# Where a weight starts in a partition: w_gate's even chunks at six new offsets past a multiple of 128 bytes

## The chip, the cores and the metric

The kernel runs on one core of one Trainium2 chip. The metric is the device time of one execution, in microseconds. A profile of one execution records the span from its first to its last instruction, each instruction's start and duration, and what released it.

## The reference

Block-causal attention over q, k and v of shape (8, 8, 576, 64) in float32, followed by a SwiGLU feed-forward layer on the 4608 tokens of 512 features that it gives:

```
scores = q @ k.T / 8, hidden where block(i) < block(j), blocks of 64
attn   = softmax(scores) @ v
x      = attn as (4608, 512)
out    = (silu(x @ w_gate) * (x @ w_val)) @ w_out
```

w_gate and w_val are (512, 1536), w_out is (1536, 512), all in 8-byte floats. The kernel keeps nearly the precision of float32 with a cheaper product type (F32R): each operand is split in a high part and a low part, and a product is the sum of three, high by high, high by low and low by high.

## The kernel before

**Tiles and loops.** The feed-forward layer works on 18 tiles of 256 tokens. The 1536 columns of w_gate and w_val are cut in 12 chunks of 128 columns, and the 512 features in 4 pieces `d` of 128. For each tile, `feed_forward` goes over the chunks in pairs (i, i+1) with i even. `up(i, 0, ...)` makes the gate products of chunk i (12 matmuls: 4 pieces by 3 products, lines 1105, 1106 and 1107) and then of chunk i+1 (12 more); `up(i, 1, ...)` does the same with w_val (24 matmuls). Each of these matmuls loads 128 by 128 weights into the array (the stationary operand, 512 bytes in each partition) and streams 256 columns of x against them (the moving operand, 1024 bytes in each partition, from `xhl`). The down product with w_out (lines 1197 to 1199) has the activations `hhl` as the stationary operand and streams 512 columns of w_out. From the fifth tile on, the 48 up matmuls of a pair stand behind each other on TensorE: 12 with an even gate chunk, 12 with an odd one, 24 with w_val. In the first four tiles the up products are cut in pieces of 3 matmuls, and attention work may stand between the pieces. Attention (lines 416 to 900) fills the time between the pairs.

**Order.** The program's order is not written out: every step is a task with a cost, a rank and buffers, and a planner (`in_order`) places the tasks on the engines before the program is built. The planner knows nothing of addresses within a partition.

**The weights.** All high and low parts of w_gate and w_val lie in SBUF for the whole run, in tiles of a pool with one buffer. `w_at(which, x, i)` gives the part x (0 high, 1 low) of chunk i. The odd chunks of w_gate are in two tiles `g_odd0` and `g_odd1` (high and low), those of w_val in `v_all0` and `v_all1`, and the even chunks of w_gate in `g_even0` and `g_even1`, with 64 bytes of an unused tile named `gap` ahead of them:

```
    half_w, whole_w = [P, NDC, DFF // 2], [P, NDC, DFF]
    g_odd = [const.tile(half_w, F32R, name=f"g_odd{x}") for x in range(2)]
    v_all = [const.tile(whole_w, F32R, name=f"v_all{x}") for x in range(2)]
    const.tile([P, 16], F32, name="gap")
    g_even = [const.tile(half_w, F32R, name=f"g_even{x}") for x in range(2)]
```

In the built program the tiles begin at these bytes of a partition: g_odd 1984 and 14272, v_all 26560 and 51136, all of them 64 past a multiple of 128; g_even 75776 and 88064, both a multiple of 128. All of `xhl`, `hhl` and the five `wo` buffers (w_out, streamed from DRAM) begin at multiples of 128. Within a tile a chunk is four runs of 512 bytes, 3072 bytes apart (6144 in v_all), so each chunk and each piece d keeps its tile's offset past a multiple of 128.

**Who writes and reads the even chunks.** `weight(i, 0)` fills a chunk once: a ScalarE cast of 128x512 writes the high part (line 983), a VectorE subtraction the low part (line 986). Before that, chunks 8 and 10 hold two pieces of w_out for a while (`AWAY`): written by the same two lines, stored to DRAM (line 1005), and streamed by a few down matmuls of the first two tiles. From then on TensorE alone reads them, in all 18 tiles.

Of the kernel before, what the change touches and what calls it, by code (L numbers as in the profile page):

```python
# [7 lines left out]
F32 = mybir.dt.float32  # L8
F32R = mybir.dt.float32r
# [9 lines left out]
def kernel(  # L19
# [21 lines left out]
    P = 128  # L41
# [5 lines left out]
    NDC = DM // P  # L47
    NFC = DFF // P
# [46 lines left out]
    const = ctx.enter_context(tc.tile_pool(name="const", bufs=1))  # L95
# [106 lines left out]
    half_w, whole_w = [P, NDC, DFF // 2], [P, NDC, DFF]  # L202
    g_odd = [const.tile(half_w, F32R, name=f"g_odd{x}") for x in range(2)]
    v_all = [const.tile(whole_w, F32R, name=f"v_all{x}") for x in range(2)]
    const.tile([P, 16], F32, name="gap")
    g_even = [const.tile(half_w, F32R, name=f"g_even{x}") for x in range(2)]

    def w_at(which, x, i):

        if which:  # L210
            return v_all[x][:, :, i * P : (i + 1) * P]
        return (g_odd if i % 2 else g_even)[x][:, :, i // 2 * P : (i // 2 + 1) * P]

# [703 lines left out]
    def weight(i, kind):  # L919
# [16 lines left out]
        def part(j):  # L936
            if wo:
                return wo[0][:, j : j + 1]
            which, c = away or (kind, i)
            return w_at(which, j, c)  # L940
# [130 lines left out]
    def feed_forward(j, t0, w, xs):  # L1071
# [19 lines left out]
        def up(i, which, prev):  # L1091
# [3 lines left out]
            for y in range(2):  # L1095

                for ds in [range(NDC)] if j >= FINE else [[d] for d in range(NDC)]:

                    def products(ds=ds, y=y):
                        hi, lo = (w_at(which, k, i + y) for k in range(2))  # L1100
                        o = ps[0][:, y * w : (y + 1) * w]
                        for d in ds:
                            xhi, xlo = (xs[d][1][k] for k in range(2))
                            first, last = d == 0, d == NDC - 1
                            nc.tensor.matmul(o, lhsT=hi[:, d], rhs=xhi[:, 0:w], start=first, stop=False)  # L1105
                            nc.tensor.matmul(o, lhsT=hi[:, d], rhs=xlo[:, 0:w], start=False, stop=False)  # L1106
                            nc.tensor.matmul(o, lhsT=lo[:, d], rhs=xhi[:, 0:w], start=False, stop=last)  # L1107

                    ts = add(
                        "PE",  # L1110
                        up_us(3 * len(ds)),
                        rank(i),
                        products,
                        [ts, *(xs[d][0] for d in ds), w_done[i + y, which]],
                        [ps, *(xs[d][1] for d in ds)],
                        stage="up",
                    )
                    ts.prev = prev
                    prev = ts if j >= FINE else None
# [336 lines left out]
```

## Time and profile before

| | us |
|---|---|
| median of 3 runs | 1174.53 |
| lowest, highest | 1172.72, 1175.42 |
| the profiled execution, its own time | 1178.6 |
| its span, first to last instruction | 1176.7 |
| TensorE matmul busy | 1149.6 |
| TensorE weight load busy | 1029.6 |
| mean granted TensorE clock | 0.991 of full speed |

Matmuls are pipelined: each one's recorded duration is longer than the distance to the start of the next, so a busy TensorE is not yet TensorE at its peak. The distance between starts is what a matmul costs in a row of them. "PE" is the matmul side of TensorE and "PEld" its weight loads, which run beside the matmul before.

### The profile page before, as it was taken

The numbers are of one execution on the slowest core, as the hardware profiler recorded it, in microseconds if no ns is written. First come the engines' busy times: TensorE is split into PE (matmuls) and PEld (weight loads), VectorE is DVE, ScalarE is ACT, GpSimd is POOL, SyncE is SP. The second block draws the span as 40 slices with busy tenths as digits, with TensorE's granted clock in tenths as the row PEclk, the third lists the DMA queues.
The fourth block names the chain that finished last, engine by engine and source line by source line (L and its number), as shares of the span: only waits on it lengthen the run. The fifth ranks groups of instructions, "written<-read, shape, count | busy, mean of one in ns | idle before, by whom it ended". The sixth has DMA issues, their size and how long they took to land.

```text
span 1176.7 us, 21979 instructions
## 1 busy us (share of the span) xinstructions
PE 1149.6 (98%) x8578; PEld 1029.6 (88%) x8578; DVE 746.6 (63%) x1230; ACT 625.0 (53%) x1114; POOL 322.1 (27%) x139
## 2 busy tenths in 40 slices
PE   6889999999999999999999999999999999999998
PEld 5567878888899998989899998989989898999997
DVE  5798889677678574768567674856648565423222
ACT  5788877646383655637374564637355463212111
POOL 3212100144523333422414332342424233000000
PEclk8899999999999999999999999999999999999999
DMA  7666858756574646755376544745556434654442
GB/s 202 168 169 189 208 178 259 190 175 175 162 180 134 172 143 172 210 176 129 132 201 199 146 150 134 216 140 163 157 161 192 166 108 148 199 160 133 146 166 103
DMA packets 266984, 197.41 MB, mean 168 GB/s; under 512 B 195264, under 2 KB 231376, under 8 KB 266880
## 3 DMA queue, kind: packets, MB, share of 16 engines
q1 hardware_dynamic: 264304, 195.29, 56.8%
q8 instruction: 67, 1.10, 0.4%
q10 hardware_dynamic: 2576, 0.72, 0.3%
q14 instruction: 37, 0.30, 0.1%
HBM read 171.57 MB, written 24.38 MB: 167 GB/s over the span
## 4 chain that ended last, share of the span: by engine, by line
PE 90%; DVE 3%; ACT 3%; DMA 2%; issue 1%; SPq 0%; POOL 0%; ACTq 0%; POOLq 0%; DVEq 0%
PE gv L1105 17%; PE gv L1107 16%; PE gv L1106 16%; PE po L1197 8%; PE po L1198 7%; PE po L1199 7%; PE at L782 7%; PE at L569 5%; PE at L653 1%; PE at L1197 1%; PE at L442 1%; PE at L1198 1%; PE at L1199 1%; DVE mx L710 1%; DMA qk<-in_k_dram 1%
## 5 line engine op out<-in xcount | busy, mean ns | idle before, releaser
L714 POOL PARTITION_ALL_REDUCE mx<-mx x80 | 141.0, 1811 | 441.7 <-DVE mx L710 131.6
L833 POOL PARTITION_ALL_REDUCE mx<-mx x48 | 178.5, 3766 | 229.1 <-DVE mx L710 210.0
L1105 PE MATMUL gv<-xhl,v_all 128*128 128x256 f32 x864 | 241.0, 279 | 0.0
L1107 PE MATMUL gv<-xhl,v_all 128*128 128x256 f32 x864 | 239.2, 277 | 0.0
L1106 PE MATMUL gv<-xhl,v_all 128*128 128x256 f32 x864 | 239.0, 277 | 0.0
L1142 DVE SCALAR_TENSOR_TENSOR t<-t,gv 128x512 f32<-128x512 f32 x108 | 73.8, 684 | 146.6 <-ACT t L1139 146.0
L1105 PEld LDWEIGHTS gv<-xhl,v_all 128*128 128x128 f32 x864 | 162.1, 188 | 3.4 <-issue 2.1
L1106 PEld LDWEIGHTS gv<-xhl,v_all 128*128 128x128 f32 x864 | 162.3, 188 | 0.8
L1155 DVE TENSOR_TENSOR hhl<-t,hhl 128x512 fp32r<-128x512 f32 x108 | 91.4, 847 | 112.3 <-ACT hhl L1152 109.0
L1107 PEld LDWEIGHTS gv<-xhl,v_all 128*128 128x128 f32 x864 | 162.2, 188 | 0.1
L1152 ACT CAST hhl<-t 128x512 fp32r<-128x512 f32 x108 | 67.3, 623 | 156.2 <-PE po L1198 114.4
L1197 PE MATMUL po<-wo,hhl 128*128 128x512 f32 x372 | 148.3, 399 | 0.7 <-ACT ob L1224 0.7
L1198 PE MATMUL po<-wo,hhl 128*128 128x512 f32 x372 | 145.6, 391 | 0.0
L1199 PE MATMUL po<-wo,hhl 128*128 128x512 f32 x372 | 145.3, 390 | 0.0
L738 DVE TENSOR_TENSOR sc<-sc,mx 128x640 f32<-128x640 f32 (+6 forms) x168 | 123.4, 774 | 20.4 <-POOL mx L714 20.4
L1139 ACT ACTIVATE t<-gv 128x512 f32<-128x512 f32 x108 | 64.6, 598 | 119.6 <-PE gv L1107 116.9
L1105 PE MATMUL gv<-xhl,g_even 128*128 128x256 f32 x432 | 124.2, 288 | 0.2 <-DVE t L1142 0.2
L742 ACT ACTIVATE sc<-sc 128x1024 f32<-128x1024 f32 (+3 forms) x104 | 105.8, 1030 | 32.5 <-DVE sc L738 31.4
L1106 PE MATMUL gv<-xhl,g_even 128*128 128x256 f32 x432 | 122.5, 283 | 0.0
L1107 PE MATMUL gv<-xhl,g_even 128*128 128x256 f32 x432 | 122.3, 283 | 0.0
L1105 PE MATMUL gv<-xhl,g_odd 128*128 128x256 f32 x432 | 120.4, 279 | 0.0
L1107 PE MATMUL gv<-xhl,g_odd 128*128 128x256 f32 x432 | 119.5, 277 | 0.4 <-DVE g_odd L986 0.4
(175 smaller groups left out, 2398.8 us busy)
## 6 DMA issues: line engine op xcount, KB each, us to landing
wo<-wo_d SPq DMA_DIRECT2D x200, 512.0 KB
out_dram<-ob SPq DMA_DIRECT2D x35, 256.0 KB
v<-in_v_dram SPq DMA_DIRECT2D x64, 128.0 KB
xt<-x_d SPq DMA_DIRECT2D x64, 128.0 KB
rt<-r_d SPq DMA_DIRECT2D x128, 64.0 KB
qk<-in_q_dram SPq DMA_DIRECT2D x112, 72.0 KB
qk<-in_k_dram SPq DMA_DIRECT2D x104, 72.0 KB
x_d<-xu SPq DMA_DIRECT2D x24, 288.0 KB
```

The costliest lines, as they stand in the source:

```text
L714: nc.gpsimd.partition_all_reduce(m, m, channels=P, reduce_op=bass_isa.ReduceOp.max)
L738: nc.vector.tensor_tensor(piece(c), scores_of(c), m, ALU.subtract)
L742: nc.scalar.activation(x, x, AF.Exp)
L782: nc.tensor.matmul(ps[0][own(x), 1 - i if sums else i, q0 - s0 : s1 - s0], lhsT=ones if sums else vt[0][:, 2 * lane + c, own(x)], rhs=sc[0 ...
L833: nc.gpsimd.partition_all_reduce(m, m, channels=P, reduce_op=bass_isa.ReduceOp.add)
L1105: nc.tensor.matmul(o, lhsT=hi[:, d], rhs=xhi[:, 0:w], start=first, stop=False)
L1106: nc.tensor.matmul(o, lhsT=hi[:, d], rhs=xlo[:, 0:w], start=False, stop=False)
L1107: nc.tensor.matmul(o, lhsT=lo[:, d], rhs=xhi[:, 0:w], start=False, stop=last)
L1155: nc.vector.tensor_tensor(hh[1][:, 0:n], t[0][:, 0:n], hh[0][:, 0:n].bitcast(F32), ALU.subtract)
L1197: nc.tensor.matmul(po, lhsT=hi, rhs=whi, start=i + y == 0, stop=False)
L1198: nc.tensor.matmul(po, lhsT=hi, rhs=wlo, start=False, stop=False)
L1199: nc.tensor.matmul(po, lhsT=lo, rhs=whi, start=False, stop=i + y == NFC - 1)
```

## The change

The six even chunks of w_gate move from the two strided tiles into one tile, and the unused tile ahead of it goes. Each chunk's high part is one run of 2048 bytes, its low part the next 2048 bytes, and each pair of parts stands at an offset of its own:

```diff
     v_all = [const.tile(whole_w, F32R, name=f"v_all{x}") for x in range(2)]
-    const.tile([P, 16], F32, name="gap")
-    g_even = [const.tile(half_w, F32R, name=f"g_even{x}") for x in range(2)]
+    past = (20, 24, 28, 36, 40, 44)
+    g_even = const.tile([P, NFC * NDC * P + 48], F32R, name="g_even")
 
     def w_at(which, x, i):
 
         if which:
             return v_all[x][:, :, i * P : (i + 1) * P]
-        return (g_odd if i % 2 else g_even)[x][:, :, i // 2 * P : (i // 2 + 1) * P]
+        if i % 2:
+            return g_odd[x][:, :, i // 2 * P : (i // 2 + 1) * P]
+        o = (i + x) * NDC * P + past[i // 2]
+        return g_even[:, o : o + NDC * P].rearrange("p (c m) -> p c m", m=P)
```

The tile begins at byte 75712, which is 64 past a multiple of 128. `past` counts words of 4 bytes, so the chunks 0, 2, 4, 6, 8 and 10 begin 16, 32, 48, 80, 96 and 112 bytes past a multiple of 128, high and low part alike, and so do their pieces d, which are now 512 bytes apart. The tiles behind it move up by 128 bytes and stay at multiples of 128; g_odd and v_all stay where they were. The instructions of every engine, their order and the semaphores and values that they wait for are the same before and after: nothing but addresses and steps of operands differs.

## The prediction, made before the changed kernel was run

> **What bounds the kernel now.** I read the page's header and its chain of waits first: they say which engine must become faster for the end to come earlier.
>
> ```profile
> span 1176.7 us, 21979 instructions
> PE 1149.6 (98%) x8578; PEld 1029.6 (88%) x8578; DVE 746.6 (63%) x1230; ACT 625.0 (53%) x1114; POOL 322.1 (27%) x139
> ...
> PE 90%; DVE 3%; ACT 3%; DMA 2%; issue 1%; SPq 0%; POOL 0%; ACTq 0%; POOLq 0%; DVEq 0%
> ```
>
> TensorE is busy for 98% of the span and holds 90% of the chain, so a nanosecond per matmul is paid almost in full at the end. The change leaves the order and the waits of every engine alone. Only the addresses of 1296 weight loads (432 in each of three lines) change, so the question is whether an address can cost TensorE time. The view of one tile's instructions (count, then shortest/median/longest duration in ns) answers that, since three groups of tiles do the same work at two offsets:
>
> ```profile
> L1105 PE MATMUL gv<-xhl,g_even x432: 277/283/580, 28.5 to 1162.9; 128*128 128x256 f32 x144
> L1106 PEld LDWEIGHTS gv<-xhl,g_even x432: 186/192/333, 28.6 to 1162.9; 128*128 128x128 f32 x144
> L1106 PE MATMUL gv<-xhl,g_even x432: 278/283/415, 28.7 to 1163.1; 128*128 128x256 f32 x144
> L1107 PE MATMUL gv<-xhl,g_even x432: 274/283/415, 28.8 to 1163.2; 128*128 128x256 f32 x144
> ...
> L1106 PEld LDWEIGHTS gv<-xhl,g_odd x432: 187/188/192, 58.9 to 1164.3; 128*128 128x128 f32 x144
> L1106 PE MATMUL gv<-xhl,g_odd x432: 276/276/282, 59.0 to 1164.4; 128*128 128x256 f32 x144
> ...
> L1106 PE MATMUL gv<-xhl,v_all x864: 274/276/284, 60.4 to 1167.2; 128*128 128x256 f32 x173
> ```
>
> Same shape, same moving operand, same engine: with weights at a multiple of 128 (g_even) a matmul's median is 283 ns and a weight load's 192; with weights 64 past it (g_odd, v_all) they are 276 and 188. Seven nanoseconds times 1296 is 9.1 us, and that is the most that the even chunks can give if the best offset seen so far is the best there is.
>
> Matmuls overlap, so I check the 7 ns by the distance between starts. The timeline of TensorE around one pair of chunks, and the sums of busy time in windows that reach from a tile's first start to the next tile's (TensorE is never idle in them, so length by count is the cost of one):
>
> ```profile
> 979.70 0.39 PE L1199 MATMUL po<-wo,hhl 128*128 128x512 f32 x1
> 979.92 0.28 PE L1105 MATMUL gv<-xhl,g_even 128*128 128x256 f32 x1
> ...
> 981.24 0.28 PE L1107 MATMUL gv<-xhl,g_even 128*128 128x256 f32 x1
> 981.36 0.28 PE L1105 MATMUL gv<-xhl,g_odd 128*128 128x256 f32 x1
> ```
> ```profile
> 979.92:981.36 1.44, 1.44 (x12) 1.00 0.16 37
> ```
> ```profile
> 981.36:982.72 1.36, 1.36 (x12) 1.00 0.97 211
> ```
>
> Twelve even matmuls take 1.44 us (120.0 ns each), the twelve odd ones behind them 1.36 (113.3): 0.08 us for each group. The granted clock is 1.00 in both.
>
> **What the offset 64 does not explain.** The same weights at the same offset do not always run at 113 ns. At 836.55 a group of 24 with v_all follows a down product directly, with no even group ahead of it; at 982.72 the like group comes behind even and odd ones:
>
> ```profile
> 836.33 0.39 PE L1199 MATMUL po<-wo,hhl 128*128 128x512 f32 x1
> 836.55 0.28 PE L1105 MATMUL gv<-xhl,v_all 128*128 128x256 f32 x1
> ...
> 839.26 0.28 PE L1107 MATMUL gv<-xhl,v_all 128*128 128x256 f32 x1
> 839.38 0.28 PE L1105 MATMUL gv<-xhl,g_even 128*128 128x256 f32 x1
> ```
> ```profile
> 836.55:839.37 2.82, 2.82 (x24) 1.00 0.52 154
> 982.72:985.44 2.72, 2.72 (x24) 1.00 1.02 375
> ```
> ```profile
> L1105 PE MATMUL gv<-xhl,v_all x8: 279/279/279, 836.5 to 839.0; 128*128 128x256 f32 x8
> L1107 PE MATMUL gv<-xhl,v_all x7: 280/280/280, 836.8 to 838.9; 128*128 128x256 f32 x7
> ```
> ```profile
> L1106 PE MATMUL gv<-xhl,v_all x8: 276/276/276, 982.8 to 985.2; 128*128 128x256 f32 x8
> ```
>
> So 64 past has two paces, 113.3 ns and 117.5 (2.82 us by 24), and whichever a row of matmuls falls into lasts to its end: shortest, median and longest agree inside each group. The slow pace is not a busier DMA: the fast window has twice its share (1.02 against 0.52). My reading is that the weight load beside a matmul and the matmul's own stream disturb each other when their fetches meet, that the start of a row decides whether they meet, and that the even chunks, at 120 ns, have so far stood at the start of nearly every row and left the 36 matmuls behind them in the fast pace. The change can thus gain at 12 matmuls of a row and lose at 36.
>
> **The change part by part.**
>
> *The even chunks' weight loads, 1296 of them.* No row shows 16, 32, 48, 80, 96 or 112 past. The nearest rows bound it: 113.3 ns is the best pace of this shape, 120.0 the worst in a settled row. If the new offsets run at 113.3, the 84 rows of the last 14 tiles (6 pairs each) give 84 x 0.08 = 6.7 us; the 24 pairs of the first four tiles, cut into pieces with attention between them, give 24 x 0.08 = 1.9 at most, of which I take two thirds: 8.0 us in all. At 117.5 the gain is 1296 x 2.5 ns = 3.2 us; a loss is not excluded, since 120 is the worst of two offsets and not of eight. If a new offset lengthened each load as much again as 192 is over 188, the loss would be 1296 x 4 ns = 5.2 us. I take 113.3: multiples of 128 make the weight load and the moving operand (xhl, at a multiple of 128 as well) begin alike, and the six new offsets are the ones at which they don't, nor begin half a period apart.
>
> *The 36 matmuls behind, 84 rows.* Unchanged in address. They stay at 113.3 (zero) or fall to 117.5: 84 x 36 x 4.2 ns = 12.7 us. In the first four tiles I count nothing. I take zero for the forecast, and 12.7 as the other end.
>
> *Fewer strides.* A weight load still reads one run of 512 bytes: nothing. The fills and the stores of w_out pieces write and read one run of 2048 bytes instead of four:
>
> ```profile
> L983 ACT CAST g_even<-wo x8: 649/668/746, 12.9 to 187.7; 128x512 fp32r<-128x512 f32 x8
> L986 DVE TENSOR_TENSOR g_even<-wo,g_even x8: 681/692/693, 13.6 to 189.0; 128x512 fp32r<-128x512 f32 x8
> L1005 SPq DMA_DIRECT2D wo_d<-g_even x4: 367/414/1649, 39.1 to 99.7; - x4
> L1002 SPq DMA_DIRECT2D wo_d<-wo x6: 326/343/452, 144.7 to 210.8; - x6
> ```
>
> Eight casts, eight subtractions and four stores in the first 200 us. Between 649 and 746 ns a cast can win or lose 0.1 us; the stores may fall from 414 ns of issue to the 343 of a store in one run, 0.3 us for four. ScalarE and VectorE are busy for 53% and 63%, and that slack hides it; without the cover it is under 1.5 us either way. I put zero. The 18 down matmuls that stream w_out from chunks 8 and 10 keep their stationary operand: at most 18 x 7 ns = 0.1 us, zero.
>
> *Sum.* -8.0 us against the profiled execution, which took 1178.6 us (span 1176.7) and lies 4.1 above the median of 1174.53. The same 1296 matmuls run in every execution, so I take the same 8.0 off the median: 1166.5 us.
>
> [...]
>
> **The rivals.**
>
> *The rows behind fall into the slow pace* (slower). Place: the first odd matmul of a row, 84 times. For it: a row that begins with clean weights at 836.55 is slow from its first matmul; the even chunks' 120 ns may be what pulls the two streams into step, and a chunk without that delay may not. Against it: an odd group at 113.3 hands a v_all group on at 113.3. Price if all six offsets do so: +12.7 less what the even chunks gain at 117.5 in those rows, 84 x 12 x 2.5 ns = 2.5: +10.2 us, 1184.7. By offset: a clean one gives -1.33 us, a bad one +1.7; with three or more bad ones of six it is slower on the whole.
>
> *Nothing, or offsets that cancel.* Two bad and four clean offsets give 2 x 1.7 - 4 x 1.33 = -1.9 us, three and three +1.1; the same if addresses do nothing at these offsets and 120 stays. For it: six offsets, each with a phase of its own, need not agree. Time: 1172.6 to 1175.6.
>
> *The new offsets are worse than 0.* +5.2 us as above, 1179.7. Against it: nothing in the trace runs a settled row above 120.
>
> *Half the gain.* Three offsets clean, three still at 120, the rest kept: -4.0, 1170.5.
>
> **How the numbers follow.** Five or six offsets clean and the fast pace kept: 0.42, with 1166.5 and a range of its own of 1164.5 to 1169. Half the gain: 0.10. No change or cancelling: 0.16. Rows behind slow at three or more offsets: 0.27; worse than 0: 0.05. About 0.2% (2.35 us) is what a measurement of this kernel tells from no change. So faster 0.52, same 0.16, slower 0.32. The low end is 1164.5, a little beyond the 9.1 us that the medians allow; the high end 1181 takes in slow rows at four or five offsets and leaves out all six.
>
> **What would show it.** Right: in the view of g_even the medians of lines 1105 to 1107 at 276 and of the weight loads at 188, a window of twelve at 1.36 us for each of the six chunks, and g_odd and v_all still at 276. Wrong: g_odd or v_all medians at 279 to 280, that is rows lost behind an even group; or 283 and more in g_even. Chunk by chunk the windows tell which offsets did it, since chunks 0 to 10 come in this order in every tile.

## The result, and the profile after

| | before | after |
|---|---|---|
| median, us | 1175.45 | 1178.52 |
| lowest, highest, us | 1172.72, 1177.46 | 1177.06, 1180.18 |
| ratio of after to before | | 1.0024, 95% interval 1.0014 to 1.0033 |
| the profiled execution, us | 1178.6 | 1179.46 |
| mean granted TensorE clock in it | 0.991 | 0.993 |

The changed kernel is slower by 2.8 us (the ratio times 1175.45; 1.6 to 3.9 by its interval), where 8.0 us less was forecast. The median of before has moved from 1174.53 to 1175.45, since it was run again beside after on the same chip. One execution of before and two of first0 in the experiments took 1271 to 1634 us at a granted clock of 0.65 to 0.85, and the ratios leave them out.

The page of after, its header and its chain of waits, answers to the first lines of the prediction:

```profile
span 1177.5 us, 21979 instructions
...
PE 1150.4 (98%) x8578; PEld 1030.7 (88%) x8578; DVE 749.1 (64%) x1230; ACT 624.4 (53%) x1114; POOL 321.7 (27%) x139
...
PE 90%; ACT 4%; DVE 2%; DMA 2%; issue 1%; POOL 0%; SPq 0%; POOLq 0%; DVEq 0%; ACTq 0%
```

TensorE bounds the kernel as before, with 98% of the span and 90% of the chain in both pages. The spans of the two profiles (1176.7 and 1177.5) can't be set against each other: the profiled execution of before is 3 us above its own median, that of after 1 us. What can be compared is the distance between the starts of matmuls. The view of one tile's instructions in after (count, shortest/median/longest ns; lines 1108 to 1110 are 1105 to 1107 of before):

```profile
L1108 PE MATMUL gv<-xhl,g_even x432: 274/280/582, 30.1 to 1163.8; 128*128 128x256 f32 x144
L1108 PEld LDWEIGHTS gv<-xhl,g_even x432: 186/188/337, 30.1 to 1163.7; 128*128 128x128 f32 x144
L1109 PE MATMUL gv<-xhl,g_even x432: 274/279/416, 30.5 to 1163.9; 128*128 128x256 f32 x144
...
L1109 PE MATMUL gv<-xhl,g_odd x432: 276/276/287, 60.0 to 1165.3; 128*128 128x256 f32 x144
...
L1109 PE MATMUL gv<-xhl,v_all x864: 276/276/287, 61.4 to 1168.0; 128*128 128x256 f32 x173
```

Of the marks that the prediction set, the weight loads came (192 to 188 ns), the matmuls did not: 279 to 280, not 276. g_odd and v_all look whole by their medians, and their longest durations tell nothing, so the windows have to be read chunk by chunk. They reach from a group's first start to the next group's first start (for v_all to its own last start, 23 distances). In after, a late tile; six rows of matmuls that stand behind a down product, chunks 0, 2, 4, 6, 8, 10, that is 16, 32, 48, 80, 96 and 112 bytes past. First the twelve matmuls with the even chunk:

```profile
963.89:965.32 1.43, 1.43 (x12) 1.00 0.19 46
972.16:973.59 1.43, 1.43 (x12) 1.00 0.25 40
980.42:981.83 1.41, 1.41 (x12) 1.00 0.35 44
994.58:995.98 1.40, 1.40 (x12) 1.00 0.23 48
1002.83:1004.23 1.40, 1.40 (x12) 1.00 0.11 37
1011.06:1012.47 1.41, 1.41 (x12) 1.00 0.27 88
```

Then, in the same six rows, the twelve with the odd chunk and the 23 distances with v_all:

```profile
965.32:966.68 1.36, 1.36 (x12) 1.00 0.83 282
973.59:974.95 1.36, 1.36 (x12) 1.00 0.91 286
981.83:983.25 1.41, 1.41 (x12) 1.00 0.75 188
995.98:997.36 1.38, 1.38 (x12) 1.00 0.91 324
1004.23:1005.59 1.36, 1.36 (x12) 1.00 0.39 136
1012.47:1013.83 1.36, 1.36 (x12) 1.00 0.94 258
...
966.68:969.29 2.61, 2.61 (x23) 1.00 0.70 226
974.95:977.56 2.61, 2.61 (x23) 1.00 0.57 231
983.25:985.95 2.71, 2.71 (x23) 1.00 1.03 381
997.36:999.96 2.61, 2.61 (x23) 1.00 0.65 205
1005.59:1008.20 2.61, 2.61 (x23) 1.00 0.97 261
1013.83:1016.44 2.61, 2.61 (x23) 1.00 0.74 247
```

No offset runs its twelve in 1.36 us: 1.40 to 1.43, by the starts in the trace 116.5 to 119.2 ns each. The row of before that the prediction read as 1.44 (120.0) is 1.434 us long by its starts, 119.5 ns each. One offset of six, 48 past in the third row, leaves the odd chunk and v_all behind it at 117.8 ns (1.41 by 12, 2.71 by 23) instead of 113.3; behind 80 past the odd chunk is in between (1.38), v_all is not.

Of the rows of 48 that nothing cuts, 77 begin behind a down product or an attention matmul. In after 17 of them end at the slow pace: all 14 of chunk 4, two others that stand behind attention, and one of chunk 0 behind a down product, at 357.33 us, where every other row of chunk 0 stays fast. The sum over the 77 (starts of their matmuls in the trace, added up by group):

| us | even | odd | v_all | last of a row | all, against before |
|---|---|---|---|---|---|
| before | 110.62 | 104.72 | 200.72 | 9.55 | |
| after | 108.99 | 105.92 | 202.45 | 9.64 | +1.38 |

So the rows are 1.4 us longer, not shorter. From the first up matmul of the fifth tile to the start of the last matmul of all, after takes 1.66 us more (816.12 against 814.46): the up products 1.39 of it, the down products 0.25, attention nothing (0.02). Whether the rest of the 2.8 lies in the first four tiles, whose rows are cut in pieces with attention between them, can't be read off: in these two profiles after reaches the fifth tile 0.84 us earlier than before, and the early attention matmuls differ by some 5 us between the profiles of this study, while the late ones agree (114.9 to 115.1 in all).

### The profile page after: what moved, and what is told of

Same layout as the page of the kernel before. It is cut to its first block, busy times and chain, and to the rows that moved or that the text cites. A ratio compares the mean times of both kernels' runs of the same rounds, so it can differ in the third digit from the quotient of the medians.

```text
span 1177.5 us, 21979 instructions
## 1 busy us (share of the span) xinstructions
PE 1150.4 (98%) x8578; PEld 1030.7 (88%) x8578; DVE 749.1 (64%) x1230; ACT 624.4 (53%) x1114; POOL 321.7 (27%) x139
## 4 chain that ended last, share of the span: by engine, by line
PE 90%; ACT 4%; DVE 2%; DMA 2%; issue 1%; POOL 0%; SPq 0%; POOLq 0%; DVEq 0%; ACTq 0%
PE gv L1108 17%; PE gv L1109 16%; PE gv L1110 16%; PE po L1200 8%; PE po L1202 7%; PE po L1201 7%; PE at L785 7%; PE at L572 6%; PE at L656 1%; PE at L1200 1%; PE at L1202 1%; PE at L1201 1%; PE at L445 1%; ACT sc L745 1%; ACT sc L463 1%
```

## The experiments

The rows of each experiment are read from one stretch of the program, the whole row that starts at 422 to 427 us behind a down product, in which before has this for its even twelve:

```profile
425.69:427.12 1.43, 1.43 (x12) 1.00 0.78 303
```

In before, the odd twelve and the 23 of v_all behind them run at 113.3 ns (1.36 and 2.61 us). Each ratio is to before, run beside it on the same chip. Where rows are counted, they are the 81 that nothing cuts: the 77 and four that follow a group with v_all.

**One offset for all six chunks.** Five versions of after differ from it only in the six numbers of `past`. They part the offsets from each other, and the positions from the new layout, since `all0` has the offset of before in the layout of after.

A mistake of mine runs through the expectations of all16 and all48: I had assigned rows to offsets by counting from the first whole row of after, at 371 us, as if it were chunk 0's. It is chunk 4's. The slow row, which I took for 16 past, is that of 48.

```diff
-    past = (20, 24, 28, 36, 40, 44)
+    past = (16,) * 6    # all0;  (20,) all16;  (28,) all48;  (0,) all64;  (40,) all96
```

> The new layout (one tile, pieces 512 bytes apart, low part right behind the high part), but all six even chunks at a multiple of 128, as before the change. Theory P (pace: only the offset past a multiple of 128 matters, and the even chunk in front of a row sets the pace of the 36 matmuls behind it): twelve even matmuls in 1.44 us, the rest of each row at 113.3 ns, about 1175.5 us, within 0.2% of before. Rival L (layout: the loss comes from the parts lying beside each other in one tile): as the changed kernel, about 1178.5 us.

Measured: 1177.67 us, ratio 1.0017 (1.0007 to 1.0028). Same offsets past 128 as before, and yet slower: the even twelve take 1.45 us where before has 1.43, and v_all behind them runs at 113.3 ns.

```profile
423.48:424.93 1.45, 1.45 (x12) 1.00 0.82 291
...
426.29:428.90 2.61, 2.61 (x23) 1.00 0.53 209
```

That looked like a price of the new layout (high beside low, runs of 2048 bytes). Two runs below say otherwise.

> All six even chunks at 16 past, the offset whose rows (chunk 0) the changed kernel runs slow to the end. Theory P: even matmuls at about 117.6 ns and all 84 whole rows at about 117.8 behind them: 84 x (36 x 4.4 - 12 x 2.4) ns = +10.9 us, about 1186 us. Rival L, or chunk 0 being slow for its place in the order and not for its offset: rows of chunks 2 to 10 stay at 113.3 behind, about 1178.5 us.

Measured: 1175.99 us, 1.0006 (0.9997 to 1.0015). One slow row of 81, again the first of the fifth tile: the expectation fell.

```profile
424.58:426.01 1.43, 1.43 (x12) 1.00 0.80 281
...
427.38:429.98 2.61, 2.61 (x23) 1.00 0.55 220
```

> All six even chunks at 48 past, the offset whose rows (chunk 4) the changed kernel runs fastest. Theory P: twelve even matmuls in about 1.40 us (116.5 ns), the rest at 113.3 with no slow tail: 108 x 12 x 3.5 ns = -4.5 us, about 1171 us. Rival L: chunk 4 is fast for its place in the order, chunk 0 stays slow behind, about 1178 us.

Measured: 1187.52 us, 1.0112 (1.0095 to 1.013). The opposite of the expectation: 80 of 81 rows are slow behind their even chunk, from the odd twelve (1.41) to the last of v_all (2.71).

```profile
423.06:424.47 1.41, 1.41 (x12) 1.00 0.63 206
...
425.88:428.59 2.71, 2.71 (x23) 1.00 0.48 191
```

> All six even chunks at 64 past, like g_odd and v_all, so that nothing stands at another offset. Theory P: rows begin in the slow pace and keep it for all 48 matmuls, as the v_all group at 836.55 us of the kernel before: 84 x (36 x 4.3 - 12 x 2.4) ns = +10.6 us, about 1186 us. Rival (64 is simply the good offset for weights): even chunks at 113.3 and the rest as well, 8 us faster than before, about 1167.5 us.

Measured: 1185.95 us, 1.0088 (1.0073 to 1.0103). With the even chunks at the same 64 past as their neighbours the whole row runs at 117.8 ns, in 77 of 81 rows: the neighbours' 113.3 ns never belonged to their offset. This is the prediction's first rival with nearly all its rows.

```profile
422.61:424.02 1.41, 1.41 (x12) 1.00 0.65 249
...
425.43:428.14 2.71, 2.71 (x23) 1.00 0.41 165
```

The other four run fast from the head on, with the same addresses. One of them, its even twelve and its v_all:

```profile
354.54:355.90 1.36, 1.36 (x12) 1.00 0.52 173
...
357.26:359.87 2.61, 2.61 (x23) 1.00 0.71 249
```

So the address does not settle the pace by itself. The down products ahead of this row start 0.236 us apart, those ahead of the other 63 rows behind a down product 0.226 to 0.228; they are also 0.236 apart ahead of the one row of chunk 0 that is slow in after. What runs ahead of a row seems to count as well; how is not shown.

> All six even chunks at 96 past in the new layout. By the traces so far the slow tail follows chunks at 48 and 64 past, and 96 is the offset whose rows are shortest: twelve even matmuls in 1.40 us (116.5 ns) and 113.3 for the 36 behind. Theory P (only the offset matters): 84 x 12 x 3.5 ns = -3.5 us, with the first four tiles -4.0, about 1171.6 us. Theory P+L (the new layout adds about 2 us at any offset, as it did at 0): about 1173.6 us.

Measured: 1174.96 us, 0.9991 (0.9982 to 0.9999). Faster, but by 1.1 us (0.1 to 2.1), because the even twelve take 1.40 us, not the 1.36 that a gain of 4 would need.

```profile
423.77:425.16 1.40, 1.40 (x12) 1.00 0.76 287
...
426.52:429.13 2.61, 2.61 (x23) 1.00 0.67 270
```

**The layout by itself.** The two strided tiles of before, moved to 96 past by a longer `gap`; 32 bytes behind them bring the tiles that follow to where all96 has them.

```diff
-    const.tile([P, 16], F32, name="gap")
+    const.tile([P, 40], F32, name="gap")
     g_even = [const.tile(half_w, F32R, name=f"g_even{x}") for x in range(2)]
+    const.tile([P, 8], F32, name="gap_behind")
```

> The layout of before (two tiles, pieces 3072 bytes apart), with g_even0 and g_even1 at 96 past. Theory P: as the new layout at 96, about 1171.6 us. Theory P+L: 2 us less than the new layout at 96, and about 4 us less than before. If the 116.5 ns belong to the new layout's addresses and not to 96, the even chunks stand at another pace here.

Measured: 1174.39 us, 0.9990 (0.9981 to 0.9998).

```profile
422.53:423.93 1.40, 1.40 (x12) 1.00 0.83 325
...
425.29:427.89 2.61, 2.61 (x23) 1.00 0.67 253
```

Old layout and new agree to 0.01 us in the sums of all 77 rows: even 108.01 and 108.02, odd 104.93 in both, v_all 200.81 and 200.82. The layout costs nothing that can be measured. This is also the lowest median found, 1.2 us (0.2 to 2.2) below before; all96 cannot be told from it.

**Tiles behind, moved by 128 bytes.** If the layout costs nothing, all0 differs from before in one thing only: the tiles behind the weights, `xhl` first of them, lie 128 bytes further. Before with nothing but that:

```diff
     g_even = [const.tile(half_w, F32R, name=f"g_even{x}") for x in range(2)]
+    const.tile([P, 32], F32, name="gap_behind")
```

> The kernel before with 128 unused bytes behind g_even, so that xhl and all tiles behind move up by 128 bytes, as they do in the changed kernel; the weights keep their old layout and place. Theory M (the distance counts modulo 256: the new layout at a multiple of 128 was slower only because xhl moved by 128): rows start at 124 ns and twelve even matmuls take 1.45 us instead of 1.43, about 1.5 us slower than before, 1177 us. Rival L (the slower rows come from the high part lying beside the low part): as before, 1175.6 us.

Measured: 1177.82 us, 1.0012 (1.0003 to 1.0021).

```profile
425.29:426.74 1.45, 1.45 (x12) 1.00 0.84 300
...
428.10:430.71 2.61, 2.61 (x23) 1.00 0.73 291
```

The 77 rows sum to those of all0 within 0.01 us: 111.44, 105.27, 200.81. So what looked like the layout's price is the shift of the tiles behind by 128, a part of the change that the prediction had not costed. It is worth 1.5 us in the whole rows, where `xhl` is the tile that moves, and 1.65 by the medians (1177.82 less the 1176.17 of before beside it). `wo` and `hhl` move as well; the down products take 0.35 us more from the fifth tile on. A multiple of 128 is not enough to say where a tile lies: `xhl` begins at 119296 in before, a multiple of 256, and at 119424 in after, 128 past one.

**Is it the weights' address, or its distance from the moving operand's?** All weights of before stay; `xhl` moves by 64 bytes, and a second gap brings `wo` and `hhl` back to multiples of 128.

```diff
     for tag, variant in first_of:
+        if tag in ("xhl", "wo"):
+            const.tile([P, 16], F32, name=f"gap_{tag}")
```

> The kernel before with one thing moved: the 16 tiles of xhl, the moving operand, stand 64 past a multiple of 128 instead of at one. Theory D (the distance between weights and moving operand counts): even chunks are now 64 apart and run at about 117.8, odd chunks and v_all are 0 apart and run at about 120: 84 x (36 x 6.7 - 12 x 2.2) ns = +18 us, about 1193.6 us. Rival A (the weights' own place in the line counts): nothing changes, about 1175.6 us.

Measured: 1193.21 us, 1.0149 (1.0134 to 1.0165), the largest effect of all, with no weight moved. Even, odd and v_all of one row:

```profile
425.42:426.83 1.42, 1.42 (x12) 1.00 0.59 176
...
426.83:428.26 1.43, 1.43 (x12) 1.00 0.88 253
...
428.26:430.99 2.73, 2.73 (x23) 1.00 0.58 236
```

So it counts here where the two operands stand to each other. That of the addresses their distance alone counts fits the runs here: at a distance of 192 a head runs at 118.0 ns here and at 117.9 in `hi64lo0` below, which gets there by moving the weights (the high parts, two loads of three). In the same way, after with `xhl` moved on by another 128 bytes, to a multiple of 256:

```diff
     g_even = const.tile([P, NFC * NDC * P + 48], F32R, name="g_even")
+    const.tile([P, 32], F32, name="gap_behind")
```

> The changed kernel with 128 more unused bytes behind g_even: xhl stands where it did before, modulo 256; chunks keep 16, 32, 48, 80, 96 and 112 past a multiple of 128. Theory M (distance modulo 256): the even chunks' paces (119.0, 119.2, 117.6, 116.8, 116.5, 117.5 ns behind a down product) change, and another chunk than the one at 48 may leave its row slow; odd chunks and v_all stand at the distance of before again. Theory 128 (distance modulo 128): the six paces stay, rows of the chunk at 48 keep 117.8 behind, time as the changed kernel, about 1178 us.

Measured: 1190.04 us, 1.0114 (1.01 to 1.0128). No weight moved here either, and now all six offsets leave slow rows:

```profile
424.73:426.14 1.42, 1.42 (x12) 1.00 0.59 179
...
427.55:430.26 2.71, 2.71 (x23) 1.00 0.57 230
```

**Who sets the pace of a row?** Three runs. `odd0` is all48 with the odd chunks moved from 64 to 0 past, to see whether a group in mid-row can bring a slow row back. The two gaps move all that lies behind them by 128, `xhl` too, so the even chunks and v_all keep their distances to `xhl`:

```diff
+    const.tile([P, 16], F32, name="gap_odd")
     g_odd = [const.tile(half_w, F32R, name=f"g_odd{x}") for x in range(2)]
+    const.tile([P, 16], F32, name="gap_v")
     v_all = [const.tile(whole_w, F32R, name=f"v_all{x}") for x in range(2)]
```

> All even chunks at 48 past, as in the run that took 1187.5 us, but the two tiles of odd chunks moved from 64 to a multiple of 128. Theory R (a group at a multiple of 128 resets the pace wherever it stands): even 117.6 ns, odd about 120, and the 24 v_all matmuls behind back at 113.3: 84 x (12 x 2.3 - 24 x 4.4) ns = -6.6 us against 1187.5, about 1181 us. Rival F (the first matmul of a row fixes its pace to the end): v_all stays at 117.8, about 1190 us.

Measured: 1189.93 us, 1.0122 (1.0108 to 1.0136). The odd twelve take 1.44 us, as an even group at distance 0 does at the head of a row, but v_all behind them stays at 2.71, in 80 of 81 rows:

```profile
427.84:429.28 1.44, 1.44 (x12) 1.00 0.92 254
...
429.28:431.99 2.71, 2.71 (x23) 1.00 0.55 222
```

In the one other row, the odd twelve and v_all:

```profile
749.77:751.22 1.45, 1.45 (x12) 1.00 0.88 281
...
751.22:753.83 2.61, 2.61 (x23) 1.00 0.74 231
```

Its even twelve are like the others' (1.42 us), so a row can come back in mid-row; it hardly ever does.

`hi64lo0` is before with the high parts at 64 past and the low parts at 0. A row then starts with a weight at 64, and its third matmul in every three has one at 0:

```diff
+    g_even = [const.tile(half_w, F32R, name="g_even0")]
     const.tile([P, 16], F32, name="gap")
-    g_even = [const.tile(half_w, F32R, name=f"g_even{x}") for x in range(2)]
+    g_even.append(const.tile(half_w, F32R, name="g_even1"))
```

> From the kernel before: the high parts of the even chunks 64 past a multiple of 128, the low parts at one; all else in place. Theory R (any weight load at a distance of 0 puts the row in the fast pace): one load in three is slowed, 12 x 4.4 ns per row, 84 x 0.053 = -4.5 us, about 1171 us. Theory F (the first matmul of a row, here at 64, fixes the slow pace to the end): 84 x (36 x 4.4 - 12 x 1.7) ns = +11.6 us, about 1187 us.

Measured: 1187.91 us, 1.0099 (1.0084 to 1.0113). Low parts at 0 don't bring the row back in 77 of the 81:

```profile
423.58:425.00 1.42, 1.42 (x12) 1.00 0.55 156
...
426.41:429.12 2.71, 2.71 (x23) 1.00 0.54 218
```

`first0` turns this round: of chunks 0, 2, 4 and 6 only the first piece (three matmuls at the head of a row) lies at 0, the other three at 64. Chunks 8 and 10 stay as they were. Their casts and subtractions are issued in two instructions each.

```diff
-    g_even = [const.tile(half_w, F32R, name=f"g_even{x}") for x in range(2)]
+    g_first = [const.tile([P, 1, 4 * P], F32R, name=f"g_first{x}") for x in range(2)]
+    g_away = [const.tile([P, NDC, 2 * P], F32R, name=f"g_away{x}") for x in range(2)]
+    const.tile([P, 48], F32, name="gap_rest")
+    g_rest = [const.tile([P, NDC - 1, 4 * P], F32R, name=f"g_rest{x}") for x in range(2)]
+    const.tile([P, 16], F32, name="gap_behind")
...
```

> From the kernel before: of the even chunks 0, 2, 4 and 6 only the first piece (d = 0, three matmuls of a row) stays at a multiple of 128, pieces 1 to 3 stand 64 past like the odd chunks; chunks 8 and 10 stay as before. Casts and subtractions of the four chunks are made in two instructions each. Theory R (the first matmuls at a distance of 0 put a row in the fast pace): nine matmuls of 56 rows at 113.3 instead of 120, 56 x 9 x 6.7 ns = -3.4 us, with the first four tiles about -4, 1171.6 us. Rival (three matmuls aren't enough, the row falls back to the slow pace): 56 x (36 x 4.4 - 9 x 2.4) ns = +7.7 us, 1183 us.

Measured: 1175.69 us, 0.9998 (0.9988 to 1.0007): no difference. Two rows show why; first the odd twelve, then v_all, each time of a row behind a down product (424 to 428) and of one behind an attention matmul (386 to 390):

```profile
424.42:425.78 1.36, 1.36 (x12) 1.00 0.93 256
386.32:387.73 1.41, 1.41 (x12) 1.00 0.83 246
...
425.78:428.38 2.61, 2.61 (x23) 1.00 0.67 259
387.73:390.44 2.71, 2.71 (x23) 1.00 0.39 154
```

Behind a down product three matmuls at 0 suffice: the even twelve take 1.37 us (114.5 ns each) and the row runs at 113.3. Behind attention three don't suffice, and the row drops to 117.8. By the starts, 1 of the 43 whole rows of chunks 0 to 6 behind a down product ends slow, and 9 of the 9 behind attention. Over the 77 rows the even groups gain 2.66 us (107.96 against 110.62), the odd and v_all groups lose 1.52 of them, and the 1.1 that are left are within the interval (a gain of 1.4 to a loss of 0.8).

This run shows one thing more, by the way. Its tiles take 256 bytes more, so `xhl` lies 256 further from g_odd and v_all than in before, and its distance from chunks 8 and 10 has changed by other multiples of 256. The 25 whole rows of these two chunks run as in before: 119.5 ns for the even twelve behind a down product (119.4 to 119.5 in before), then 113.3 and 113.3, behind attention as well. A shift of 128 had changed them (before_up128), one of 256 does not.

## Why the prediction was wrong

**The step that failed first: "I take 113.3" for the new offsets.** They took 116.5 to 119.2 ns. The value came from g_odd and v_all, and all64 shows that it is not theirs by position: with the even chunks at the same 64 the whole row runs at 117.8 in 77 of 81 rows. The 113.3 ns of the groups behind are what a head of a row at a favourable distance leaves, and that head itself, at 116.5 to 121.4 ns, pays for it. The prediction said nearly this ("the even chunks, at 120 ns, have so far stood at the start of nearly every row and left the 36 matmuls behind them in the fast pace") and then priced the gain as if pace were a matter of the offset. The gain that was there, 1.6 us over 77 rows (110.62 less 108.99), stands where 77 x 0.08 = 6.2 were put.

**Bounds that were read too narrowly.** The prediction calls 120.0 ns the worst pace in a settled row and says that nothing in the trace runs above it. In 12 of the 13 whole rows of before that stand behind attention the even twelve take 1.46 us, 121.4 ns each:

```profile
387.61:389.06 1.46, 1.46 (x12) 1.00 1.14 282
```

And by its own prices five bad offsets come to 1181.7, so its high end of 1181 takes in four, not five.

**The step that was missing: the shift of the tiles behind.** The section on the change and the prediction took "a multiple of 128" for a full description of an address. before_up128 makes the shift alone cost 1.65 us by the medians, with a ratio clear of 1 (1.0003 to 1.0021). Over the 77 rows it adds 0.82 us in before's even groups, 0.55 in the odd ones and 0.09 in v_all.

**The rows behind.** Their loss was right in kind, in pace (117.8 measured, 117.5 taken) and in price: 1.41 + 2.71 less 1.36 + 2.61 is 0.15 us for a row of chunk 4 (the prediction's 36 x 4.2 ns). The forecast took none of 84; 17 of the 77 whole rows do it, 2.6 us. In the sums that is the larger part of +1.20 in odd and +1.73 in v_all. The rival in its full form, all offsets bad, put 1184.7; all64 came to 1185.95 and after_up128 to 1190.04.

**Steps that held.** The layout, with its other strides in fills and stores, costs nothing measurable (old96 against all96, before_up128 against all0); no wait has become the bound, with PE at 90% of the chain as before. The busier DMA is not what slows a row: in after the slow v_all window has a share of 1.03, a fast one 0.97.

**The reading behind the price.** That a weight load and the stream beside it disturb each other when their fetches meet was the prediction's own reading, and no run shows it. What is measured is that their places matter together: xhl64 moves one of the two operands by 64 bytes and costs 17.6 us (1193.21 less 1175.60). Why is not shown.

**What adds up and what doesn't.** By whole rows the change is worth +1.38 us: the shift of `xhl` +1.47, the chunks' new distances -2.45 in their own groups and +2.36 behind them. The stretch from the fifth tile on gives +1.66. The measured loss is 2.8 (1.6 to 3.9), so 1.1 us stay unassigned; they lie in the first four tiles' cut rows or in the width of the measurement, and nothing here tells which. The same stretch, read in each run's profile against before's, falls inside the interval of the measured time in all 13 kernels: +1.9 us in all0 and before_up128, -1.9 in all96 and old96, +10.8 in all64, +16.0 in xhl64.

## What to carry to other kernels

Read a matmul's pace in a row from the whole row, its head and its tail, and never credit a group with a pace that the group ahead of it has set. Describe an operand's place by its distance from the other operand, modulo 256 bytes here, and treat a padding that "keeps alignment" as a change of its own, to be run alone. Where rows are long and TensorE is the bound, trying a gap of some tens of bytes is cheap: the runs of this case spread from 1174.4 to 1193.2 us by addresses alone.

## What the runs showed of the hardware

The table gives the distance of the even chunk's weights from the moving operand in bytes, modulo 256, and the pace that it leaves for the odd chunk and v_all behind it, in nearly all rows behind a down product. The exceptions are one or two of the 64 in a run, those named above among them.

| distance at the head of a row | even twelve, ns | behind it, ns | from |
|---|---|---|---|
| 0 | 119.4 | 113.3 | before |
| 128 | 120.8 | 113.8, then 113.3 | all0, before_up128 |
| 144, 160 | 119.0, 119.2 | 113.8 and 113.3, then 113.3 | after; 144 also all16 |
| 176 | 117.6 (odd0 118.1) | 117.8 | after, all48; head of odd0 |
| 208 | 116.8 | 114.7, then 113.3 | after |
| 224, 240 | 116.5, 117.5 | 113.3 and 113.6, then 113.3 | after; 224 also all96, old96 |
| 16, 32, 48, 80, 96, 112 | 117.4 to 119.7 | 117.8 | after_up128 |
| 64 | 117.8 | 117.8 | all64 |
| 192, low parts at 0 | 117.9 | 117.8 | hi64lo0 |

Shape and granted clock (1.00) are the same in all of them. Groups at 64 (after, all64) or 192 (before, hi64lo0, after_up128) behind the head have two lasting paces, 113.3 and 117.8 ns; in these runs the head of the row, and what runs ahead of it, picks one, and they keep either. In xhl64 the head is at 192 and takes 118.0 ns, the groups behind it are at 128 and take 118.5 to 119.0. A period of 256 bytes fits what was tried: shifts of 128 changed the paces (the even twelve from 119.4 to 120.8 ns in before_up128; the pace of v_all behind five chunks of six from 113.3 to 117.8 in after_up128), the shift of 256 in first0 did not (119.5 and 113.3 in chunks 8 and 10, as before); and odd0, where the even weights and `xhl` both stand 128 further than in all48, keeps the head's pace (118.1 against 117.6) and the 117.8 behind it. Open: why a head at distance 0 brings a row to the quick pace while a group at 0 in mid-row does so in one row of 81 (odd0), why three matmuls at 0 suffice behind a down product and not behind attention (first0), and why a row can be quick with all its weights at 64 (all64).

The product type F32R took 0.44 ns for each column streamed (113.3 ns for the 256 of an up matmul at the quick pace), F32 0.84: the attention products of line 782, which are in F32, start in pairs of 64 weight columns each, and from pair to pair 320 columns take 269 ns (before, the median by the starts). No run has an up matmul in F32, so what it would take is not shown.
